# Batch 0 of a sparse attention and MoE kernel, taken pair by pair, with its loads cut to match and a few planned steps moved

## The chip, the cores and the metric

The kernel runs on one core of one Trainium2 chip. The metric is device time in microseconds of one execution (us); lower is better. Engines are named as the profile does: PE (matrix multiplication), PEld (PE's weight loads), DVE (vector), ACT (scalar, with the exponential and logarithm), POOL (GpSimd, which also issues most of the loads) and SP (which issues the stores and some transposes). DMA engines move data between HBM and on-chip memory.

## The reference, cut to what matters

An attention with two kinds of masks, then a two-layer MoE block without routing.

```python
batch, n_heads, seq, head_dim = (8, 8, 576, 64)
stride = 32
rel = pos[:, None] - pos[None, :]
mask_local = (rel >= 0) & (rel < stride)                     # heads 0 to 3
mask_strided = (rel >= 0) & (pos[None, :] % stride == pos[:, None] % stride)   # heads 4 to 7
scores = np.where(masks, scale * q @ k.T, -1e9)
attn = softmax(scores)
x = (attn @ v)  # heads side by side: 4608 tokens x 512
h = x @ w_in            # 512 x 2048
g = np.maximum(h, 0.0) ** 2
out = g @ w_out         # 2048 x 512, float32
```

All inputs are float32 in HBM; the kernel computes in bfloat16, and the loads that POOL issues change the type on the way.

## The kernel before, in words

**Tiles.** Heads go in pairs: a unit u = 4 * batch + pair is two heads of one batch. Pairs 0 and 1 are local, pairs 2 and 3 strided. The attention's output for pair p of all batches lies transposed in `xt[p]` (128 rows = two heads of 64, one column for each of the 4608 tokens). The MoE then runs over nine chunks of 512 tokens. For a chunk, `mm1(c, ff)` (L740) makes one of 16 blocks ff of the hidden layer: four matmuls, one for each pair kk, against `w_in_b`, summed in one bank of PSUM; ACT applies the ReLU, DVE squares. `mm2` (L843) multiplies the squares by `w_out_b` in quarters: part 0 needs the first quarter of w_out, part 1 the second, and so on.

**The order of work is written by hand.** Every engine runs its own instructions in program order. First comes a set-up (L975 to L1015), then batch 0 as the list of words `BATCH0` (L18), each run by `run_step` (L879), then the groups: one group is one `mm1` (four matmuls) or four matmuls of `mm2`, and `PLAN` (L23) says which words of the attention of later batches are put ahead of which group. Groups 0 to 4 are empty, since their blocks were made in batch 0's list; groups 5 to 15 are blocks ff 5 to 15 of chunk 0, groups 16 to 31 its `mm2` (16 to 19 with the first quarter of w_out, 20 to 23 with the second), and from 32 on chunk 1.

**The words that matter here.** A number after a slash gives the PSUM banks.
- `c0q`: change the type of a local pair's q or k on ACT (a), DVE (v) or POOL (g); `T0q`: six transposes on PE and a copy.
- `W0q0`: transposes of the strided q or k of batch 0 in two halves (12 transposes of 96 rows each and a copy, L343 to L352); for later batches (`W1q0`, L334) eight transposes of 72 rows.
- `b2.0`: a bias that carries the mask, written to PSUM by PE (L512); `S2.0`: half of a pair's scores (L542) and the exponential on ACT (L546).
- `N2`: the row sums of a strided pair by PE, then ACT's logarithm and exponential (L660 to L664); `O2`: its product with V and DVE's multiplication into `xt` (L674, L676).
- `H0`: a shift of 32 rows in local V (L447); `D0`: a local pair's product with V, DVE's reciprocal and multiplication (L689 to L696); `E0`: transposes and a copy into `xt` (L729, L732).
- `P0.01`: the matmuls of `mm1` for pair 0 and blocks ff 0 and 1. All 20 matmuls of blocks 0 to 4 are done in this way, in the order of pairs 0, 2, 1, 3.
- `z`: DVE makes the wide local mask for later batches; `w1`: a matmul on nothing, to keep PE warm.
- Of the plan: `l` loads a local q or k, `r` a strided one of batch 1, `V` local V, `U` strided V (two loads), `o` a quarter of w_out, all issued by POOL; `m` are fills by POOL; `s1.x` strided scores of batch 1, `x1.x` its sums and products with V (L617): first the sum with `ones_bd` (L622), then eight or six products with `vb` (L625); `B10`, `B11` spread strided V into `vb` (L434); `D4.0` one half of unit 4's product with V (L699).

**The loads.** SP loads pair 0's q and k. All other loads are issued by POOL, one after another, and go through one queue. Before the change they are: strided q (L324), strided k, pair 1's q and k (L306), local V (L440), strided V (L649), w_in in four parts (L462; blocks ff 0 to 4 for pairs 0 and 2, the same for pairs 1 and 3, blocks 5 to 10, blocks 11 to 15), then those of the plan.

Batch 0 is done with the two local and the two strided pairs interleaved: strided scores before pair 1's, and outputs of pairs 0 and 1 before those of 2 and 3.

Of the kernel before, what the change touches and what calls it, by code (L numbers as in the profile page):

```python
# [9 lines left out]
BF16 = mybir.dt.bfloat16  # L10
# [16 lines left out]
4: r1k V1  # L27
5: o1 U1 mbg
6: o2 l2k8+9 mv0g o3 mk0g
10: c4qv  # L30
11: c4kv
12: l2q8+9 T4qa c5qv
# [135 lines left out]
def kernel(  # L168
# [21 lines left out]
    NBS = 2 * NJ  # L190
    VP = 72
    SR = 80
    NP2 = STRIDE // 2
# [22 lines left out]
    strTs = {nm: rows.enter_context(tc.tile_pool(name=f"strT{nm}", bufs=n, side="right")) for nm, n in (("q", 2), ("k", 1))}  # L216
# [26 lines left out]
    ident = singles.tile([128, 128], BF16)  # L243
# [31 lines left out]
    st = {}  # L275
# [40 lines left out]
    NP3 = 4 * SP_ // QL  # L316
    str_rows = {}

    def load_str_rows(b, name):
        src = q if name == "q" else k  # L320
        if b == 0:
            c = 4 if name == "q" else 8
            t = w_out_b[0:QL, c:c + NP3, :]
            nc.gpsimd.dma_start(out=t, in_=src[b, 4:8].rearrange("h (p j) d -> (h p) (j d)", j=NJ)  # L324
                                .rearrange("(s p) c -> p s c", p=QL))
        else:
            t = str_rows_t[name][0:SP_]
            nc.gpsimd.dma_start(out=t, in_=src[b, 4:8].rearrange("h (m r) d -> (h m) (r d)", r=STRIDE))
        str_rows[b, name] = t

    def step_TS(b, name, g, copy):
        src = str_rows[b, name]
        pt = bank("pt").bitcast(BF16)[:, 0:S]
        if b:  # L334
            for i in range(NJ):
                c = 128 * (NJ * g + i)
                nc.tensor.transpose(pt[:, SP_ * i:SP_ * (i + 1)], src[:, c:c + 128], ident[0:SP_, 0:SP_])  # L337
            if g == 0:
                o = strTs[name].tile([128, NP2 * SR], BF16, name=f"{name}T_s")
                str_T[b, name] = o.rearrange("c (a p) -> c a p", p=SR)  # L340
            copy(str_T[b, name][:, NJ * g:NJ * (g + 1), 0:SP_], pt.rearrange("c (a p) -> c a p", p=SP_))
            return
        for i in range(2):  # L343
            for s3 in range(NP3):
                c = 128 * (2 * g + i)
                o = S // 2 * i + QL * s3
                nc.tensor.transpose(pt[:, o:o + QL], src[:, s3, c:c + 128], ident[0:QL, 0:QL])
        if g == 0:
            o = strTs[name].tile([128, 2 * NJ * SR], BF16, name=f"{name}T_s")
            str_T[b, name] = o[:, 0:2 * NJ * SP_].rearrange("c (a r) -> c a r", a=NJ // 2)  # L350
        o = str_T[b, name]
        copy(o[:, 2 * g:2 * g + 2, :].rearrange("c a r -> c (a r)"), pt)  # L352
        if g == 1:
            for i in range(2):
                st.setdefault(2 + i, {})[name + "T"] = \
                    o[:, :, 2 * SP_ * i:2 * SP_ * (i + 1)].rearrange("c a (h p) -> c h a p", h=2)

    str_T = {}

# [77 lines left out]
    def load_v_local_sw(b):  # L437
        i = (2 * b) % NV
        t = vl_all[:, i:i + 2]
        nc.gpsimd.dma_start(out=t[32:128, :, :, :, 0:D].rearrange("p u h t d -> p (u h t) d"),  # L440
                            in_=v[b, 0:4].rearrange("h (t p) d -> p (h t) d", p=QL))
        for u in range(2):
            st.setdefault(4 * b + u, {})["v"] = t[:, u]
# [13 lines left out]
            st.setdefault(4 * b + u, {})["v"] = t[:, u]  # L457

    def load_w_in(i):
        f = slice(*((0, 640), (0, 640), (640, 1344), (1344, 2048))[i])  # L460
        c = (slice(0, 4, 2), slice(1, 4, 2), slice(0, 4), slice(0, 4))[i]
        nc.gpsimd.dma_start(out=w_in_b[:, c, f], in_=w_in_v[:, c, f])  # L462

    def load_w_out(i):
# [182 lines left out]
    def load_v0():  # L647
        load_v_local_sw(0)
        nc.gpsimd.dma_start(  # L649
            out=vs0.rearrange("p u n d -> p (u n d)").rearrange("p (h c) -> p h c", h=4),  # L650
            in_=v[0, 4:8].rearrange("h (p j) d -> p h (j d)", j=NJ))

    def step_N(u):
        e, hw = st[u]["e"], S // 2
# [217 lines left out]

    idle = xt[0][:, T - 512:T]

    def first_part(kks, ffs):
        for ff in ffs:
            mm1(0, ff, kks, FIRST, None if ff < 2 else "py")

    def run_step(word):  # L879
        word, _, at = word.partition("/")  # L880
        places[:] = [int(x) for x in at.split(",") if x]
        op, arg = word[0], word[1:]
        if op == "w":
            warm(int(arg))
        elif op == "c":
            cast_qk_local(int(arg[:-2]), arg[-2], ENG[arg[-1]])
        elif op == "T":
            step_T(int(arg[:-2]), arg[-2], ENG[arg[-1]])
        elif op == "W":
            step_TS(int(arg[0]), arg[1], int(arg[2]), ENG[arg[3]])  # L890
        elif op == "S":
            u, _, half = arg.rstrip("!").partition(".")
            step_S(int(u), int("!" in arg), [int(half)] if half else range(2))
        elif op == "G":
            step_G(int(arg))
        elif op == "b":
            step_B(*(int(x) for x in arg.split(".")))
        elif op == "N":
            step_N(int(arg))
        elif op == "O":  # L900
            step_O(int(arg))
        elif op in "sx":
            (step_SS if op == "s" else step_XX)(*(int(x) for x in arg.split(".")))
        elif op == "k":
            step_K(int(arg[0]), int(arg[1]), ENG[arg[2]])
        elif op == "m":
            memset_later(arg[:-1], nc.gpsimd if arg[-1] == "g" else nc.vector)
        elif op == "D":
            if "." in arg:
                u, part = arg.split(".")  # L910
                step_D(int(u), int(part))
            else:
                step_D0(int(arg))
        elif op == "E":
            step_E(int(arg.rstrip("av")), ENG.get(arg[-1]))
        elif op == "P":
            first_part(*([int(x) for x in y] for y in arg.split(".")))
        elif op == "H":
            shift_v_local(int(arg[:-1]), ENG[arg[-1]])
        elif op == "C":  # L920
            load_str_tall(int(arg[:-1]), arg[-1])
        elif op == "Q":
            load_qk_rows(int(arg[:-1]), arg[-1])
        elif op == "X":
            transpose_str(int(arg[:-1]), arg[-1])
        elif op == "A":
            transpose_cast(int(arg[:-1]), arg[-1])
        elif op == "R":
            order_local(int(arg[:-2]), arg[-2], ENG[arg[-1]])
        elif op == "Y":  # L930
            transpose_local(int(arg))
        elif op == "V":
            (load_v_local_sw if int(arg) > 2 else load_v_local_all)(int(arg))
        elif op == "U":
            load_v_str(int(arg))
        elif op == "B":
            spread_v_str(int(arg[0]), int(arg[1]), ENG[arg[2]])
        elif op == "l":
            load_qk_local_sw(int(arg[0]), [int(x) for x in arg[2:].split("+")], arg[1])
        elif op == "r":  # L940
            load_str_rows(int(arg[0]), arg[1])
# [60 lines left out]
    for i in range(2):  # L1002
# [92 lines left out]
```

## Time and profile before

| | |
|---|---|
| median of 3 runs | 296.94 us (296.74 to 297.06) |
| the profiled execution: time | 297.07 us |
| its span, first to last instruction | 295.2 us |
| busy: PE, DVE, ACT, POOL | 286.3, 210.5, 170.7, 83.0 us |
| instructions | 5895 |
| read from HBM, written | 37.22 MB, 9.44 MB |

A row of the timeline gives the start in us from the span's start, the duration, engine, line, operation, what it writes `<-` what it reads, shape and count (merged instructions: the duration is from the first's start to the last's end); in brackets the idle time of the engine just before, and what ended it. A row of the chain of waits gives start, duration and what ran. A row of the DMA view names a load, its size as it lands (KB) and the median time from issue to landing. The times of the profiled execution lie 1.87 us above its span; the rest of the execution is outside of all instructions.

### The profile page before, as it was taken

Reading aid. Unit: us, or ns where it says so; the run is one execution under the profiler, and the core shown is the slowest. Engines: PE = TensorE matmul, PEld = TensorE weight load, DVE = VectorE, ACT = ScalarE, POOL = GpSimd, SP = SyncE. Lnnn points to the kernel's source line nnn. Section 1 sums busy time; section 2 is a strip of 40 time slices with the busy share of each in tenths; the row PEclk is TensorE's granted clock in tenths of the full one; section 3 lists DMA queues with packets and bytes.
Section 4 is the critical chain, followed back from the end, with each engine's and each line's share of the span. In section 5 each row is a group of like instructions: output and inputs, shape, how many; then the busy total and the mean of one; then the engine's idle time right before and its main releaser. Section 6 shows DMA issues by size and latency. Waiting matters only on the chain.

```text
span 295.2 us, 5895 instructions
## 1 busy us (share of the span) xinstructions
PE 286.3 (97%) x2177; PEld 155.7 (53%) x2212; DVE 210.5 (71%) x553; ACT 170.7 (58%) x321; POOL 83.0 (28%) x123
## 2 busy tenths in 40 slices
PE   7899999999999999999999999999999999999995
PEld 3554555545545454554454445544454444894594
DVE  6557687697666759678367835675489969968983
ACT  3758846775668736774577447645665466307610
POOL 8874743004513008119303800000000013102300
PEclk9999999999999999999999999999999999999999
DMA  7999999999999999999999999411011110021003
GB/s 149 188 207 204 192 198 190 150 204 215 147 138 213 117 163 201 136 166 141 216 159 147 165 186 147 83 56 73 36 23 52 58 54 0 1 104 42 0 2 142
DMA packets 91724, 37.38 MB, mean 127 GB/s; under 512 B 77548, under 2 KB 85830, under 8 KB 91696
## 3 DMA queue, kind: packets, MB, share of 16 engines
q0 software_dynamic: 50608, 18.33, 57.2%
q1 hardware_dynamic: 40944, 18.62, 34.3%
q8 instruction: 17, 0.28, 0.4%
q14 instruction: 11, 0.09, 0.1%
q10 hardware_dynamic: 144, 0.07, 0.1%
HBM read 37.22 MB, written 9.44 MB: 158 GB/s over the span
## 4 chain that ended last, share of the span: by engine, by line
PE 94%; DMA 2%; issue 1%; DVE 1%; ACT 0%; POOL 0%; DVEq 0%; POOLq 0%
PE psb L748 42%; PE psb L854 33%; PE psb L824 9%; DMA w_out_b<-in_k_dram 2%; PE psb L707 2%; PE psb L625 1%; PE psb L611 1%; PE psb L622 1%; PE psb L587 1%; PE psb L542 1%; PE psb L490 1%; PE psb L729 0%; PE psb L512 0%; PE psb L337 0%; DVE x_l L696 0%
## 5 line engine op out<-in xcount | busy, mean ns | idle before, releaser
L748 PE MATMUL psb<-xt,w_in_b 128*128 128x512 bf16 x557 | 131.7, 379 | 1.1
L754 ACT ACTIVATE r<-psb 128x512 bf16<-128x512 f32 x144 | 85.4, 599 | 47.2 <-PE psb L748 41.8
L854 PE MATMUL psb<-w_out_b,g_sb 128*128 128x512 bf16 x432 | 100.9, 379 | 1.1 <-issue 0.5
L748 PEld LDWEIGHTS <-w_in_b 128*128 128x128 bf16 x576 | 53.2, 97 | 58.3 <-issue 0.9
L758 DVE TENSOR_TENSOR g_sb<-r 128x512 bf16<-128x512 bf16 x112 | 47.1, 423 | 37.0 <-ACT r L754 36.1
L854 PEld LDWEIGHTS <-g_sb 128*128 128x128 bf16 x448 | 41.0, 97 | 44.7
L793 POOL CAST sa<-g_sb 128x256 fp32r<-128x256 bf16 x16 | 9.7, 607 | 100.3 <-DVE g_sb L788 100.3
L638 DVE TENSOR_TENSOR xt<-psb,rv 64x144 bf16<-64x144 f32 x84 | 26.2, 311 | 11.5 <-ACT rv L630 10.4
L858 ACT COPY y<-psb 128x512 f32<-128x512 f32 x28 | 16.6, 592 | 29.4 <-PE psb L854 28.4
L628 ACT ACTIVATE rv<-psb 128x432 f32<-128x432 f32 (+1 forms) x21 | 10.5, 501 | 12.8 <-PE psb L622 12.8
L713 DVE TENSOR_TENSOR x_l<-psb,rinv 96x384 bf16<-96x384 f32 x28 | 15.5, 553 | 1.0
L365 POOL DMA_DIRECT2D q_t<-in_q_dram x6 | 3.4, 569 | 45.3 <-DMA qT_s<-q_t 44.0
L788 DVE TENSOR_TENSOR g_sb<-r 128x512 bf16<-128x512 bf16 x32 | 13.0, 420 | 3.7 <-ACT r L754 3.7
L598 ACT ACTIVATE e<-psb 128x384 bf16<-128x384 f32 x30 | 12.0, 510 | 4.2 <-PE psb L587 4.2
L594 DVE TENSOR_TENSOR e<-e,mask_all 128x576 bf16<-128x576 bf16 x20 | 8.4, 456 | 7.3 <-ACT e L598 7.2
L294 POOL DMA_DIRECT2D k_l<-in_k_dram x16 | 12.2, 765 | 3.6 <-DMA v_st<-in_v_dram 3.6
L612 ACT ACTIVATE e<-psb 128x432 bf16<-128x432 f32 (+1 forms) x21 | 10.4, 496 | 4.0 <-PE psb L611 4.0
L645 DVE TENSOR_TENSOR xt<-psb,rv 64x270 bf16<-64x270 f32 (+1 forms) x28 | 9.8, 425 | 3.7 <-ACT rv L630 3.5
L824 PE MATMUL psb<-t,s 128*128 128x256 f32 x96 | 12.2, 283 | 0.0
L294 POOL DMA_DIRECT2D q_l<-in_q_dram x16 | 11.6, 728 | 0.7 <-DMA k_l<-in_k_dram 0.7
L824 PEld LDWEIGHTS psb<-t,s 128*128 128x128 f32 x96 | 11.6, 189 | 0.0
L630 ACT ACTIVATE rv<-rv 128x432 f32<-128x432 f32 (+1 forms) x21 | 11.2, 532 | 0.7
(135 smaller groups left out, 311.0 us busy)
## 6 DMA issues: line engine op xcount, KB each, us to landing
out_dram<-y SPq DMA_DIRECT2D x35, 256.0 KB, 3.8
w_out_b<-in_moe_w_out_dram POOLq DMA_DIRECT2D x4, 512.0 KB, 15.3
q_t<-in_q_dram POOLq DMA_DIRECT2D x7, 288.0 KB, 7.2
k_t<-in_k_dram POOLq DMA_DIRECT2D x7, 288.0 KB, 6.8
vl<-in_v_dram POOLq DMA_DIRECT2D x6, 288.0 KB, 7.3
v_st<-in_v_dram POOLq DMA_DIRECT2D x7, 216.0 KB, 7.8
w_in_b<-in_moe_w_in_dram POOLq DMA_DIRECT2D x2, 704.0 KB, 13.8
k_l<-in_k_dram POOLq DMA_DIRECT2D x16, 72.0 KB, 7.8
```

The costliest lines, as they stand in the source:

```text
L294: nc.gpsimd.dma_start(out=t[:, :, hh, :], in_=src[b, 2 * p + hh].rearrange("(t p) d -> p t d", p=QL))
L598: nc.scalar.activation(e[:, row, 4 * QL * i:4 * QL * (i + 1)], bk[row][i][:, 0:4 * QL], AF.Exp, scale=scale)
L630: nc.scalar.activation(rv, rv, AF.Exp, scale=-1.0)
L638: nc.vector.tensor_tensor(to[:, :, NJ * part:NJ * (part + 1), par], of, by, op=ALU.mult)
L713: nc.vector.tensor_tensor(x, po[0:QL, :, 0:D], rinv[0:QL].to_broadcast([QL, NL, D]), op=ALU.mult)
L748: nc.tensor.matmul(ph, w_in_b[:, kk, 128 * ff:128 * (ff + 1)], xt[kk][:, 512 * c:512 * (c + 1)], start=(kk == order[0]), stop=(kk == order ...
L754: nc.scalar.activation(r, ph, AF.Relu)
L758: later(1, lambda: nc.vector.tensor_tensor(g[:, ff, :], r, r, op=ALU.mult))
L788: nc.vector.tensor_tensor(g[:, ff, :], r, r, op=ALU.mult)
L824: nc.tensor.matmul(pa, a, b, start=k == 0 and n not in "273", stop=k == 7, skip_group_check=True)
L854: nc.tensor.matmul(py, g[:, ff, 128 * j:128 * (j + 1)], w_out_b[:, ff, :], start=(ff == 0), stop=(ff == 15))
L858: nc.scalar.copy(y, py)
```

## The change

Batch 0's list is written anew: pair 1's q and k come in ahead of the strided ones, scores go pair 0, pair 1, pair 3, pair 2 in half units, then D1, D0, N3, E1, O3, N2, E0, O2, and the 20 matmuls of blocks 0 to 4 are single words `P<pair><block>` in an order that begins with pair 1. The order of the four pairs within a block follows from the list. `z` moves behind most of them and the warming matmuls go. The loads of batch 0 follow a list of their own: strided q, k and V by pairs (two heads on 72 rows), local V by pairs, the two first parts of w_in in exchanged order with pair 2's strided V between them, and the rest of w_in in three parts in place of two. The shift of local V is done by pairs too (`h1`, `h0`).

In the plan `o1` (the second quarter of w_out) goes ahead of `V1` (batch 1's local V), `o3` ahead of the next batch's k, and the words D4, D5, B10, B11, E4 and x1.0 come one or two groups later.

```diff
-FIRST = (0, 2, 1, 3)
+LOADS = "k1 q1 sq3 sk3 sk2 sq2 vl1 vl0 vs3 w1 vs2 w0"
 BATCH0 = """
-    c0qa c0kv T0qa/6 w1/7 T0kv/4 z w1/7 S0/0,2 W0q0v/4 W0q1v/5 b2.0/0 W0k0v/6 W0k1a/7 b2.1/2 b3.0/4 S2
-    c1qv c1kv T1qv/6 T1kv/7 S3.0 b3.1/0 S3.1 b1.0/2 S1.0 b1.1/6 S1.1 H0v D0/4 N2/0 D1/6 E0a/4 N3/2 O2/0
-    P0.01 E1a/6 P0.2/7 P2.012 O3/2 P0.34/0,1 P2.34 P1.01234 P3.0 P3.1 P3.2 P3.3 P3.4
+    c0qa c0kv b1.0/2 T0qa/1 T0kv/6 c1kv S0.1/4 c1qv S0.0/6 T1kv/1 T1qa/5 t3qv/4 b1.1/6 t3kv/0 S1.1 S1.0 t2kv/5
+    b3.1/0 t2qv/4 S3.1 b2.0/2 h1v b3.0/6 h0v S2.0 D1/4 S3.0 b2.1/0 S2.1 D0/2 N3/6 E1v/4 O3/0 N2/6 E0a/2 P10/4
+    P11/5 P14/3 O2/6 P31 P12/0 P33/1 P34 P32 P30 P22 P20 P21 P13 P24 P01 z P00 P02 P04 P23 P03
 """
-4: r1k V1
-5: o1 U1 mbg
-6: o2 l2k8+9 mv0g o3 mk0g
+4: r1k o1
+5: V1 U1 mbg
+6: o2 o3 l2k8+9 mv0g mk0g
...
-19: C2q C2k V2 k11v D4.0
-20: s1.0 D4.1 B10v
-21: s1.1 D5.0
-22: B11v l3k12+13 s1.2 U2
-23: E4a D5.1
-24: x1.0
+19: C2q C2k V2 k11v
+20: s1.0
+21: s1.1 D4.0
+22: D4.1 l3k12+13 s1.2 U2
+23: D5.0 B10v
+24: E4a D5.1 B11v
+25: x1.0
...
+    def load_str_unit(u, name):
+        src = q if name == "q" else k
+        c = (4 if name == "q" else 8) + 2 * (u - 2)
+        t = w_out_b[0:SP_, c:c + 2, :]
+        nc.gpsimd.dma_start(out=t, in_=src[0, 2 * u:2 * u + 2].rearrange("h (p j) d -> p h (j d)", j=NJ))
+        str_rows[u, name, 0] = t
+
+    def step_TU(u, name, copy):
+        src = str_rows[u, name, 0]
+        pt = bank("pt").bitcast(BF16)[:, 0:S]
+        for i in range(NJ):
+            h, a = divmod(i, NJ // 2)
+            nc.tensor.transpose(pt[:, SP_ * i:SP_ * (i + 1)], src[:, h, 128 * a:128 * (a + 1)], ident[0:SP_, 0:SP_])
...
     def load_w_in(i):
-        f = slice(*((0, 640), (0, 640), (640, 1344), (1344, 2048))[i])
-        c = (slice(0, 4, 2), slice(1, 4, 2), slice(0, 4), slice(0, 4))[i]
+        f = slice(*((0, 640), (0, 640), (640, 1024), (1024, 1536), (1536, 2048))[i])
+        c = slice(i, 4, 2) if i < 2 else slice(0, 4)
...
+    def load_v0_local(u):
+        t = vl_all[:, u]
+        nc.gpsimd.dma_start(out=t[32:128, :, :, 0:D].rearrange("p h t d -> p (h t) d"),
+                            in_=v[0, 2 * u:2 * u + 2].rearrange("h (t p) d -> p (h t) d", p=QL))
+        st.setdefault(u, {})["v"] = t
+
+    def shift_v0(u, copy):
+        t = vl_all[:, u]
+        copy(t[0:32, :, 1:NL, 0:D], t[96:128, :, 0:NL - 1, 0:D])
+
+    def load_v0_str(u):
+        nc.gpsimd.dma_start(out=vs0[:, u - 2].rearrange("p (h c) d -> p h (c d)", h=2),
+                            in_=v[0, 2 * u:2 * u + 2].rearrange("h (p j) d -> p h (j d)", j=NJ))
...
-    def first_part(kks, ffs):
-        for ff in ffs:
-            mm1(0, ff, kks, FIRST, None if ff < 2 else "py")
+    parts = [w.partition("/")[0][1:] for w in BATCH0.split() if w[0] == "P"]
+
+    def first_part(kk, ff):
+        mm1(0, ff, [kk], [int(x[0]) for x in parts if int(x[1]) == ff])
...
     load_qk_hw(0)
-    load_str_rows(0, "q")
+    loads = (LOADS + " w2 w3 w4").split()
+    load_first(loads[0])
     make_identity(nc, ident)
-    load_str_rows(0, "k")
+    load_first(loads[1])
...
-    load_qk_local_sw(0, (1,))
-    load_v0()
-    for i in range(4):
-        load_w_in(i)
+    for word in loads[2:]:
+        load_first(word)
```

In the list of loads `k1` and `q1` are pair 1's, `sq3` the strided q of pair 3, `vl1` local V of pair 1, `vs3` strided V of pair 3, `w1` and `w0` the parts of w_in for pairs 1 and 3 and for pairs 0 and 2.

More of the change, by code (lines that the diff above doesn't have):

```diff
@@ L314, in cast_qk_local @@
         s[name] = t
-    NP3 = 4 * SP_ // QL
     str_rows = {}
@@ L320, in load_str_rows @@
         src = q if name == "q" else k
[L321 to L328, printed above, removed]
-        str_rows[b, name] = t
+        t = str_rows_t[name][0:SP_]
+        nc.gpsimd.dma_start(out=t, in_=src[b, 4:8].rearrange("h (m r) d -> (h m) (r d)", r=STRIDE))
+        str_rows[b, name] = t
+    def load_str_unit(u, name):
[10 more added lines that the diff above has]
+            nc.tensor.transpose(pt[:, SP_ * i:SP_ * (i + 1)], src[:, h, 128 * a:128 * (a + 1)], ident[0:SP_, 0:SP_])
+        if (0, name) not in str_T:
+            str_T[0, name] = strTs[name].tile([128, NP2 * SR], BF16, name=f"{name}T_s")
+        o = str_T[0, name][:, S * (u - 2):S * (u - 1)]
+        copy(o, pt)
+        st.setdefault(u, {})[name + "T"] = o.rearrange("c (h a p) -> c h a p", h=2, p=SP_)
     def step_TS(b, name, g, copy):
@@ L333, in step_TS @@
         pt = bank("pt").bitcast(BF16)[:, 0:S]
[L334 to L347, printed above, removed]
-        if g == 0:
[L349 to L356, printed above, removed]
+        for i in range(NJ):
+            c = 128 * (NJ * g + i)
+            nc.tensor.transpose(pt[:, SP_ * i:SP_ * (i + 1)], src[:, c:c + 128], ident[0:SP_, 0:SP_])
+        if g == 0:
+            o = strTs[name].tile([128, NP2 * SR], BF16, name=f"{name}T_s")
+            str_T[b, name] = o.rearrange("c (a p) -> c a p", p=SR)
+        copy(str_T[b, name][:, NJ * g:NJ * (g + 1), 0:SP_], pt.rearrange("c (a p) -> c a p", p=SP_))
     str_T = {}
@@ L645, in step_XX, with load_first @@
                     nc.vector.tensor_tensor(t, of[:, g:, :, lo:lo + k], by[:, g:, :, lo:lo + k], op=ALU.mult)
[L647 to L651, printed above, removed]
+    def load_v0_local(u):
[9 more added lines that the diff above has]
+                            in_=v[0, 2 * u:2 * u + 2].rearrange("h (p j) d -> p h (j d)", j=NJ))
+    def load_first(word):
+        if word[0] == "w":
+            load_w_in(int(word[1]))
+        elif word[0] == "v":
+            (load_v0_local if word[1] == "l" else load_v0_str)(int(word[2]))
+        elif word[0] == "s":
+            load_str_unit(int(word[2]), word[1])
+        else:
+            load_qk_local_sw(0, (int(word[1]),), word[0])
     def step_N(u):
@@ L890, in run_step @@
             step_TS(int(arg[0]), arg[1], int(arg[2]), ENG[arg[3]])
+        elif op == "t":
+            step_TU(int(arg[0]), arg[1], ENG[arg[2]])
+        elif op == "h":
+            shift_v0(int(arg[0]), ENG[arg[1]])
         elif op == "S":
@@ L916, in run_step @@
         elif op == "P":
-            first_part(*([int(x) for x in y] for y in arg.split(".")))
+            first_part(int(arg[0]), int(arg[1]))
         elif op == "H":
```

## The prediction

> **What bounds the kernel now.** I read the page's slices first, then the timeline of the first 50 us, then the DMA view in short windows, last the chain of waits.
>
> ```profile
> PE   7899999999999999999999999999999999999995
> DMA  7999999999999999999999999411011110021003
> ```
>
> PE is busy nine tenths or more of every slice (7.4 us each) but the first two and the last. So an edit to batch 0 can win only what PE idles in front, and keeps it only if nothing later makes PE wait again. The second line warns of that: the DMA engines are full from the second slice to the 25th. Two stretches decide. First, the timeline where the first part of the MoE's first chunk (the 20 matmuls of the P steps) runs, and a row of the chain:
>
> ```profile
> 10.11 0.46 DVE L352 COPY kT_s<-psb 128x576 bf16<-128x576 bf16 x1 [0.98 <-PE psb L347]
> 11.28 3.56 ACT L546 ACTIVATE e<-psb 72x576 bf16<-72x576 f32 x6 [0.35 <-PE psb L542]
> 13.23 0.48 DVE L447 COPY vl<-vl 32x1280 bf16<-32x1280 bf16 x1
> 14.72 0.23 DVE L695 RECIPROCAL rinv<-psb 96x12 f32<-96x12 f32 x1 [1.01 <-PE psb L689]
> 15.03 0.65 ACT L662 ACTIVATE g_sb<-psb 128x576 f32<-128x576 f32 x1 [0.19 <-PE psb L660]
> 15.71 0.68 ACT L664 ACTIVATE g_sb<-g_sb 128x576 f32<-128x576 f32 x1
> 15.86 0.22 DVE L695 RECIPROCAL rinv<-psb 96x12 f32<-96x12 f32 x1
> 16.46 0.64 ACT L732 COPY xt<-psb 128x576 bf16<-128x576 bf16 x1
> 18.80 0.45 PE L674 MATMUL psb<-e,g_sb 72*64 72x72 bf16 x16
> 19.36 0.76 DVE L676 TENSOR_TENSOR xt<-psb,g_sb 128x576 bf16<-128x576 f32 x1 [1.44 <-PE psb L674]
> ...
> 19.25 5.07 PE psb L748 x23
> ```
>
> From 11.28 ACT goes from exponentials (3.56/6 = 0.59 us each) to sums (0.65 + 0.68 a pair) to copies (0.64), and PE's chunk matmuls wait for it. From 19.25 (the chain's row) PE runs through at 5.07/23 = 0.22 us a matmul; 14 of the 20 are after 19.25, so **ff 5 starts at 19.25 + 14 x 0.22 = 22.3**.
>
> Second, the loads. POOL's queue is served in the order of issue; these are issues (timeline) and times to landing (DMA view, windows up to 14 us):
>
> ```profile
> 1.37 0.85 POOL L324 DMA_DIRECT2D w_out_b<-in_q_dram  x1 [0.86 <-POOLq L1079]
> 4.26 0.67 POOL L306 DMA_DIRECT2D xt<-in_q_dram  x1
> 5.65 1.18 POOL L440 DMA_DIRECT2D vl<-in_v_dram  x1
> 6.82 0.75 POOL L649 DMA_DIRECT2D g_sb<-in_v_dram  x1
> 7.57 2.99 POOL L462 DMA_DIRECT2D w_in_b<-in_moe_w_in_dram  x4
> 10.54 0.69 POOL L306 DMA_DIRECT2D xt<-in_q_dram  x1
> 13.54 0.55 POOL L328 DMA_DIRECT2D q_t<-in_q_dram  x1 [0.62 <-DMA vl<-in_v_dram]
> ...
> xt<-in_q_dram POOLq DMA_DIRECT2D x1, 144.0 KB, 6.0
> vl<-in_v_dram POOLq DMA_DIRECT2D x1, 288.0 KB, 7.3
> g_sb<-in_v_dram POOLq DMA_DIRECT2D x1, 288.0 KB, 8.0
> w_in_b<-in_moe_w_in_dram POOLq DMA_DIRECT2D x1, 320.0 KB, 8.8
> q_t<-in_q_dram POOLq DMA_DIRECT2D x1, 288.0 KB, 16.5
> ...
> 30.29 0.51 PEld L337 LDWEIGHTS <-q_t 72*128 72x128 bf16 x8
> ```
>
> Landings: q1 10.3, local V 12.95, strided V 14.8, the first part of w_in 16.4, and batch 1's strided q (q_t) at 13.54 + 16.5 = 30.0. PE takes q_t (W1q0v, group 14) at 30.29. **That load is only 0.25 us early.** Whatever PE wins before it beyond that, it loses waiting there, unless the queue moves up as well.
>
> **Part 1: batch 0 pair by pair.** The three strided loads and local V are halved, w_in is cut in five: 15 issues for 10, the same bytes. At about 0.75 us an issue (2.99/4) POOL is busy 5 x 0.75 = 3.7 us longer, and l1q4, issued at 10.54 before, goes out near 14.2. The row at 13.54 shows what hides that: a load waits for the eighth before it, so some seven are always queued, and q_t takes 16.5 us to land.
>
> What the order costs is at the queue's head. Rows of the DMA view for 2 to 4, 4 to 6, 6 to 8 and 16 to 18 us (packets, MB, share):
>
> ```profile
> q0 software_dynamic: 9, 0.01, 3.6%
> q0 software_dynamic: 271, 0.27, 105.9%
> q0 software_dynamic: 365, 0.34, 115.5%
> q0 software_dynamic: 312, 0.42, 118.2%
> ```
>
> Before 4 us POOL's queue moved 9 packets although its first load was issued at 1.37: some 2.4 us pass before data flows. By 6.0 it had moved 0.28 MB. The new order has only k1 and q1 (2 x 144 KB, 0.295 MB) issued by then, so it is empty at about 6.1; the next load leaves POOL at 4.1 to 4.3, behind the mask operations as q1 did before, and moves from about 6.5. **The queue loses about 0.4 us** (none, if k1 is slow to start; 0.6 at most).
>
> The 72-row halves are the unknown. Strided V, 288 KB on 72 rows, took 14.82 - 12.95 = 1.87 us of the queue; at the rate of the fourth row (0.21 MB/us) it would be 1.42. The three loads that become 72-row halves (strided q, k, V) are 2 x 1.42 + 1.87 = 4.7 us at those prices. Six halves cost 6 x 0.71 = 4.3 if they fill one another's gaps fully, 6 x 0.94 = 5.6 if not at all: -0.4 to +0.9. I take zero: at the third row's 0.17 MB/us, which held while strided q and k moved, the old three come to 2 x 1.73 + 1.87 = 5.3, near the upper end, and some filling closes the rest. So loads of equal position land L = 0.4 later, bounds -0.4 to +1.5.
>
> [...]
>
> Walked through with L = 0.4: the four strided halves, k1 and q1 together have the bytes up to the old k1, which stood 0.7 behind q1's 10.3; so the last half lands at 11.4, local V at 12.4 and 13.4, strided V of pair 3 14.3, w1 15.9, pair 2 16.8, w0 18.4.
> - DVE: h0v waits for 13.4 and takes 0.24 (half of the row at 13.23); then D1 and D0 at 1.14 each (from one reciprocal to the next): to 16.0. E1v's copy as the row at 10.11, with latency 0.5: 16.5, and P10 at **16.8**.
> - ACT: after the last half, transposes and copy, about 0.9, to 12.3; four exponentials to 14.8; N3 1.33 to 16.2; N2 after its matmuls to 17.7; E0a to 18.4; O2's multiply on DVE, 0.76 from 18.0, to 18.8.
> - PE: 20 x 0.22 + 0.45 for O2 = 4.85 from 16.8. P31 is due at 17.9 (pair 3 ready 17.3), P22 at 19.2 (18.8; w0 18.4), P01 at 20.3 (18.4): no hole. **ff 5 at 21.6, 0.7 earlier.**
>
> W0's 48 transposes become 32 and the warming matmuls go; both lie ahead of P10 where PE has holes, and count nothing. "z" on DVE lies ahead of the first squares. w_in's last part lands near 25.4 and is due at 21.6 + 7 x 0.88 = 27.8.
>
> At W1q0v q_t now lands at 30.4; PE would come at 29.6. It starts L - 0.25 = **0.15 us later than before**. The gain in front is spent.
>
> **Part 2: the plan.**
>
> ```profile
> 21.94 0.76 POOL L466 DMA_DIRECT2D w_out_b<-in_moe_w_out_dram  x1 [1.27 <-PE psb L748]
> vl<-in_v_dram POOLq DMA_DIRECT2D x1, 384.0 KB, 16.8
> w_out_b<-in_moe_w_out_dram POOLq DMA_DIRECT2D x1, 512.0 KB, 16.6
> 38.89 1.03 PE L854 MATMUL psb<-w_out_b,g_sb 128*128 128x512 bf16 x4
> ```
>
> Second quarter of w_out: landed 38.5, used 38.89, 0.4 early. Ahead of V (384 KB, about 1.9 us) it lands near 37, V near 38.9 in its place; D4.0, now in group 21, comes at 39.8 or later. Neither waits. The swap saves nothing as long as PE does not come earlier.
>
> The later steps have a price. D5.1 and B11v now stand in group 24, x1.0 in group 25; before, B11v was two groups ahead of x1.0.
>
> ```profile
> 42.32 0.52 DVE L434 COPY vb<-v_st 54x1408 bf16<-54x1408 bf16 x1
> 43.11 0.18 DVE L712 RECIPROCAL rinv<-psb 96x6 f32<-96x6 f32 x1
> 43.33 0.55 DVE L713 TENSOR_TENSOR x_l<-psb,rinv 96x384 bf16<-96x384 f32 x1
> ...
> 42.62 0.86 PE psb L854 x4
> 43.48 0.18 PE psb L622
> ```
>
> After D5.1 PE has four matmuls, 0.86, and x1.0's sum, 0.18; x1.0's products with vb (L625) are due 1.04 us after D5.1's end. On DVE after that end: 0.1 until the reciprocal, 0.7 for both steps, 0.5 for B11v, some 0.1 to PE: 1.4. **PE waits 0.35 us** (0 if DVE's steps overlap more; 0.6 if DVE is behind). Everything of PE stands behind it in its queue.
>
> **The sum** against the profiled execution (297.07 = span 295.2 + 1.87): +0.15 + 0.35 = +0.5. The median of the runs shown is 0.13 lower, 296.94; so **297.4**, +0.17%. About 0.2%, 0.6 us, is what a measurement of this kernel tells from no change.
>
> **Rivals.**
> - **The queue moves up and the gain stays** (faster). Early loads flowed at 0.17 MB/us (third row), not 0.21. If the halves of strided q and k (0.59 MB) run at the later rate, 0.6 is saved, and 0.4 if all six fill their gaps: L = 0.4 - 1.0 = -0.6, q_t at 29.4, and PE wins 0.85. With B11v's wait hidden 296.1, paid 296.45. For: strided V, later in the queue, fits the full rate. Against: the slow rows are the queue's first, whatever stands there. Chance 0.25, of it 0.2 faster.
> - **The halves do not share engines** (slower). L = 0.4 + 0.9 = 1.3: q_t at 31.3, +1.05, and B11v +0.35: 298.3. It decides from L = 0.5, where both waits make +0.6. For: strided V's 1.87. [...] Chance 0.15.
> - **As forecast**, two small waits, 296.9 to 297.9: chance 0.6, of it 0.2 over +0.6.
> [...]
>
> **Numbers.** Predicted 297.4; range 296.2 to 298.3, from the gain kept to the halves unshared, some 0.1 left out on each side. Faster by over 0.2%: 0.2. Within: 0.05 + 0.4 = 0.45. Slower: 0.15 + 0.2 = 0.35.
>
> **What would show it.** In the new trace: the first matmul of L748 near 16.8 and ff 5 near 21.6; q_t landing after 30.2 and PE waiting for it; the second w_out quarter long landed when used, D4.0 without a wait; an idle piece of PE before x1.0's L625 put down to vb. I am wrong if q_t lands before 29.8 (then faster), if ff 5 starts after 22.5 (a wait in batch 0 that I did not see), or if PE waits for V or v_st in groups 21 to 25.

## The result, and the profile after

The changed kernel takes **301.94 us** (median of 4 runs, 301.02 to 305.78) against 297.0 for the kernel before: a ratio of 1.0157, 95% interval 1.0124 to 1.0189. The forecast was 297.4 with a range up to 298.3. It is slower by 1.6%, where +0.17% was forecast. Ratios here and below leave out executions that were disturbed, so a ratio can differ from that of two medians.

The profiled execution is the longest of the four, 305.78 us. Its slices (page, second part; 7.6 us each):

```profile
PE   7898999999949999999999999999999999999995
PEclk9999999999987999999999999999999999999999
DMA  7999999999999999999999999821112110011003
```

Against the rows of before there is one hole in PE, in the twelfth slice, and right behind it a dip of the clock. What PE waited for behind the first 18 us (view of waits, up to 120 us; us in total, times, longest):

```profile
PE psb L763 <- DMA xt<-x_l: 4.0, 1, 4.0
PE psb L487 <- DVE q_l L314: 0.6, 1, 0.6
PE psb L622 <- DVE vb L431: 0.4, 1, 0.4
PE psb L487 <- DVE k_l L314: 0.4, 1, 0.4
```

The first row is what this execution has beyond the others, with a stretch at half clock behind it (windows of 5 us; the granted clock stands behind the engines' busy times):

```profile
85.00:90.00 5.00, 1.05 (x5) 0.31 (x4) 3.17 (x7) 2.78 (x5) 1.43 (x2) 0.86 1.62 102
90.00:95.00 5.00, 5.00 (x12) 1.73 (x12) 0.85 (x2) 1.49 (x3) 0.00 (x0) 0.50 1.72 134
```

The first experiment comes back to it. The other three waits are the change's own. The timeline shows who waits for whom; DVE and PE in turn, then POOL's issue of batch 1's strided q and its time to landing:

```profile
28.27 0.36 DVE L314 COPY q_l<-xt 96x768 bf16<-96x768 bf16 x1 [0.86 <-DMA xt<-in_q_dram]
29.92 0.36 DVE L314 COPY k_l<-xt 96x768 bf16<-96x768 bf16 x1 [0.96 <-DMA xt<-in_k_dram]
...
28.69 0.43 PE L487 MATMUL psb<-ident,q_l 96*128 96x96 bf16 x6 [0.64 <-DVE q_l L314]
30.33 0.43 PE L487 MATMUL psb<-ident,k_l 96*128 96x96 bf16 x6 [0.35 <-DVE k_l L314]
45.88 0.39 PE L622 MATMUL psb<-e,vb 128*128 128x54 bf16 x8 [0.36 <-DVE vb L431]
...
16.88 0.55 POOL L322 DMA_DIRECT2D q_t<-in_q_dram  x1 [0.30 <-POOL q_t L990]
...
q_t<-in_q_dram POOLq DMA_DIRECT2D x1, 288.0 KB, 14.4
```

POOL's queue is late: batch 1's local q and k land when DVE starts on them, 28.25 and 29.9 (before 26.67 and 27.98), and strided q lands at 16.88 + 14.4 = **31.3** (before 30.0, forecast 30.4). So PE already waits two groups ahead of the place the prediction named. The 0.36 us before x1.0's products stands where it was forecast (0.35).

Most other executions of the same kernel look different. The kernel once more (`same_again`), windows of 5 us: PE, PEld, DVE, ACT, POOL busy (instructions), then the granted clock, DMA share, GB/s; and the kernel before in two of them:

```profile
5.00:10.00 5.00, 4.14 (x73) 2.93 (x71) 3.47 (x7) 2.82 (x5) 5.00 (x7) 1.00 1.03 131
10.00:15.00 5.00, 4.21 (x60) 2.94 (x60) 2.13 (x6) 2.32 (x5) 4.87 (x7) 0.72 1.51 147
15.00:20.00 5.00, 4.89 (x59) 3.05 (x59) 2.97 (x5) 3.50 (x6) 4.19 (x6) 0.50 1.22 196
20.00:25.00 5.00, 4.89 (x32) 2.15 (x32) 0.76 (x1) 1.18 (x3) 4.36 (x5) 0.76 1.25 207
```

```profile
5.00:10.00 5.00, 3.81 (x55) 2.55 (x54) 2.42 (x6) 1.88 (x3) 4.98 (x7) 1.00 1.30 168
10.00:15.00 5.00, 4.92 (x91) 3.16 (x89) 3.27 (x8) 4.16 (x7) 4.26 (x6) 1.00 1.57 196
```

PE reads as busy through most of it, but **its clock fell to a half from 12.2 to 22.4 us** (the column behind the engines: 0.72, 0.50, 0.76; in these windows busy time is that of slowed matmuls: four matmuls of the chunk take 1.91 us at half clock, at 23.35 in `small_first`, and 1.03 at full clock, at 35.65 there). Behind it PE waits for no load at all, since it comes 3.4 us late itself:

```profile
31.63 0.43 PE L487 MATMUL psb<-ident,q_l 96*128 96x96 bf16 x6
```

This is PE's first work for batch 1's local q (block ff 12); in the kernel before it starts at 28.25. The row makes a good milestone: it parts what PE loses ahead of it, in front, from what it waits for behind it. (ff 5, forecast at 21.6 and a sign of being wrong after 22.5, starts at 22.05 in the first profile and at 25.7 in this one; before at 22.4.) The mean clock of a whole execution tells the two kinds apart: it was 0.977 to 0.983 in six of the eight executions of the changed kernel. Of the other two, one is the first profile (0.989), and one, 302.45 us at 1.0, has none.

### The profile page after: what moved, and what is told of

Same layout as the page of the kernel before. It is cut to its first block, busy times and chain, and to the rows that moved or that the text cites. A ratio compares the mean times of both kernels' runs of the same rounds, so it can differ in the third digit from the quotient of the medians.

```text
span 303.8 us, 5912 instructions
## 1 busy us (share of the span) xinstructions
PE 289.9 (95%) x2183; PEld 156.4 (51%) x2218; DVE 211.5 (70%) x555; ACT 170.4 (56%) x320; POOL 86.0 (28%) x128
## 4 chain that ended last, share of the span: by engine, by line
PE 82%; DMA 10%; POOL 4%; issue 2%; DVE 1%; ACT 0%; DVEq 0%; SPq 0%; POOLq 0%
PE psb L763 38%; PE psb L869 27%; PE psb L839 9%; DMA xt<-x_l 5%; DMA xt<-in_k_dram 5%; PE psb L722 2%; PE psb L608 1%; POOL w_in_b L459 1%; PE psb L622 1%; PE psb L584 1%; PE psb L619 1%; POOL w_out_b L329 1%; PE psb L487 1%; POOL vl L646 1%; PE psb L539 1%
## 5 line engine op out<-in xcount | busy, mean ns | idle before, releaser
L763 PE MATMUL psb<-xt,w_in_b 128*128 128x512 bf16 x557 | 134.5, 384 | 5.1 <-DMA xt<-x_l 4.0
L625 ACT ACTIVATE rv<-psb 128x432 f32<-128x432 f32 (+1 forms) x21 | 10.5, 501 | 12.6 <-PE psb L619 12.6
L839 PE MATMUL psb<-t,s 128*128 128x256 f32 x96 | 12.2, 283 | 0.0
## 6 DMA issues: line engine op xcount, KB each, us to landing
w_out_b<-in_moe_w_out_dram POOLq DMA_DIRECT2D x4, 512.0 KB, 14.8
```

What stands on the lines that cost most here:

```text
L763: nc.tensor.matmul(ph, w_in_b[:, kk, 128 * ff:128 * (ff + 1)], xt[kk][:, 512 * c:512 * (c + 1)], start=(kk == order[0]), stop=(kk == order ...
L839: nc.tensor.matmul(pa, a, b, start=k == 0 and n not in "273", stop=k == 7, skip_group_check=True)
```

## The experiments

Three theories stood after this. **The halves**: the 72-row loads cost the queue time, the recorded slow rival. **The clock**: the new list leaves PE so little to do early on that its clock falls, and the queue does not matter. **The gap**: the thinner head of the queue (k1 and q1, then nothing) is what makes it late. The table has all runs; milestones in us from each profile: "k" is the landing of batch 1's local k, "q_t" that of its strided q, "ff 12" PE's first work for its local q (the wait right before it left out), "waits" what PE waits for from there up to 50 us. A wait ahead of ff 12 is not in the last column; it shows in ff 12.

| kernel | median us (range, runs) | ratio (95%) | profiled: us, clock | k | q_t | ff 12 | waits |
|---|---|---|---|---|---|---|---|
| before | 296.94 | | 297.07, 1.0 | 28.0 | 30.0 | 28.25 | 0 |
| changed | 301.94 (301.02–305.78, 4) | 1.0157 (1.0124–1.0189) | 305.78, 0.989 | 29.9 | 31.3 | 28.05 | 1.35 |
| same_again | 301.41 (300.95–302.38, 4) | 1.0148 (1.0124–1.0173) | 301.15, 0.982 | 29.5 | 31.0 | 31.63 | 0.4 |
| old_plan | 301.02 (298.93–304.29, 6) | 1.0120 (1.0088–1.0152) | 298.93, 1.0 | 29.1 | 30.5 | 27.9 | 1.8 |
| new_plan | 297.28 (297.05–302.53, 12) | 0.9996 (0.9971–1.0022) | 297.06, 1.0 | 27.5 | 29.1 | 27.7 | 0.3 |
| head_one | 302.83 (301.2–305.95, 6) | 1.0195 (1.0152–1.0238) | 301.2, 0.982 | 30.75 | 32.2 | 31.7 | 0.4 |
| warm_list | 301.88 (300.38–302.96, 6) | 1.0145 (1.0112–1.0178) | 300.38, 0.998 | 30.4 | 31.8 | 28.6 | 2.5 |
| before_no_warm | 297.47 (296.58–303.5, 12) | 1.0006 (0.9986–1.0026) | 296.86, 0.999 | 28.8 | 30.2 | 28.05 | 0 |
| halves_old_order | 301.52 (300.12–302.61, 4) | 1.0151 (1.0115–1.0186) | 300.12, 0.997 | 30.1 | 31.3 | 28.9 | 1.6 |
| small_first | 304.23 (303.73–304.58, 4) | 1.0228 (1.0200–1.0257) | 304.2, 0.977 | 28.5 | 29.9 | 35.0 | 0.4 |
| half_qk | 299.84 (299.08–304.05, 6) | 1.0080 (1.0061–1.0099) | 300.29, 0.994 | 30.75 | 31.6 | 31.4 | 0 |
| half_v | 298.33 (296.94–303.83, 12) | 1.0041 (1.0016–1.0066) | 303.48, 0.994 | 27.7 | 29.25 | 28.3 | 0.4 |
| half_v_again | 300.11 (297.57–304.24, 10) | 1.0026 (1.0009–1.0042) | 298.12, 0.998 | 28.7 | 29.8 | 27.8 | 0.3 |
| five_w_in | 297.14 (297.01–297.58, 11) | 0.9994 (0.9979–1.0008) | 297.26, 1.0 | 28.7 | 30.1 | 28.1 | 0.2 |
| whole_loads | 298.19 (297.8–306.08, 9) | 1.0031 (1.0019–1.0042) | 298.3, 1.0 | 29.0 | 30.2 | 29.1 | 0.4 |
| half_qk48 | 298.16 (297.31–303.81, 12) | 1.0033 (1.0011–1.0056) | 297.31, 0.999 | 28.55 | 30.3 | 28.3 | 0 |
| after48 | 301.56 (300.86–304.73, 6) | 1.0172 (1.0133–1.0212) | 301.76, 0.982 | 29.75 | 31.1 | 31.5 | 0.4 |
| after48_warm | 298.99 (298.54–300.61, 6) | 1.0069 (1.0048–1.0091) | 298.8, 0.999 | 29.15 | 30.2 | 28.4 | 1.1 |

**1. The kernel once more** (`same_again`, no edit).

> The changed kernel as it is, for a second profile and more times. Its first profile has three losses: PE waits 1.2 us for batch 1's local q and k (groups 10 to 13), 0.4 us for vb before x1.0, and near 86 us 4.0 us for the transposing DMA that brings unit 9's output into xt, after which the granted clock is 0.5 for 5 us. If the third is what sets runs apart, this profile shows the first two again at about the same size, and the third with another one; if the time is 301 to 302 with no third loss, the theory of three losses is wrong.

Measured: 301.41 us, without the 4 us hole, without the waits for q and k, and with the clock at a half in front. By its own terms the theory of three losses was wrong. So the hole at 85 us is a thing of single executions. In the first profile it came from one of SP's transposes of `x_l` into `xt` (issue, and time to landing; that profile first, then before):

```profile
74.14 3.82 SPq L737 DMA_TRANSPOSE xt<-x_l  x1
...
xt<-x_l SPq DMA_TRANSPOSE x1, 15.6
```

```profile
70.68 1.26 SPq L722 DMA_TRANSPOSE xt<-x_l  x1
...
xt<-x_l SPq DMA_TRANSPOSE x1, 8.1
```

It landed at 89.8 instead of 78.8. A like row stands in `half_v`'s profile (1.7 us, and 2.1 for a transpose of q_t). Why these transposes are late at times is not settled.

**2. The two halves of the change apart** (`old_plan`: the changed kernel with the plan of before; `new_plan`: the kernel before with the changed plan).

> Batch 0 and its loads as changed, the plan as before (second quarter of w_out behind V1, D4 to x1.0 at the old groups). Queue theory (the new loads make POOL's queue 1.3 to 1.9 us late, everything else follows): the waits for local q and k stay at 1.2 us, the wait for vb goes (0.4 us), a wait for the second quarter of w_out may come, and the late transposes stay: 300 to 302 us. Plan theory (the later steps of the plan make the late loads late): no wait near 86 us, 297.5 to 298.5 us.

> Batch 0 and its loads as before, only the plan as changed. Queue theory: the queue is on time, so only the wait for vb before x1.0 is paid, 0.3 to 0.4 us: 297.3 to 297.5 us, and the transposes of unit 9 come in time. Plan theory: most of the loss is here, 300 us or more, with PE waiting near 86 us.

The plan alone is no loss that can be measured, 0.9996, though its profile has the wait for vb:

```profile
PE psb L626 <- DVE vb L435: 0.3, 1, 0.3
```

That it is paid is seen, what it comes to in the total is inside the interval. Nearly all of the loss comes with batch 0 and its loads. And with the late queue the old plan is no better by more than the intervals allow (1.0120 against 1.0157): in its profile PE waits for the second quarter of w_out, which the changed plan had brought forward:

```profile
PE psb L868 <- DMA w_out_b<-in_moe_w_out_dram: 1.5, 1, 1.5
```

**3. The gap at the head** (`head_one`: the first strided half is issued right behind q1, ahead of the masks).

```diff
     load_first(loads[1])
+    load_first(loads[2])
...
-    for word in loads[2:]:
+    for word in loads[3:]:
```

> The changed kernel with the first strided load (sq3) issued right behind q1, ahead of the mask operations on POOL, so that the queue is not empty between q1 and sq3; the masks come 0.7 us later. Gap theory (the queue is late because it ran empty at its head): batch 1's local k lands 0.5 to 0.8 us earlier than 29.9 and the wait of PE in groups 10 to 13 falls from 1.2 to about 0.5 us. Halves theory (the 72-row halves are slow in themselves): it lands less than 0.3 us earlier.

With the gap filled q_t lands at 32.2, later than ever. **The gap theory falls** as the cause of the late queue. The 0.4 us that the prediction took for the gap is not seen at q_t in `small_first` either (29.9, experiment 5).

**4. The clock kept up** (`warm_list`: eight matmuls on zeros in the changed list; `before_no_warm`: the two warming steps, one matmul each, taken out of the list before, as the change does).

```diff
-... T0qa/1 T0kv/6 c1kv S0.1/4 c1qv S0.0/6 T1kv/1 T1qa/5 t3qv/4 b1.1/6 t3kv/0 S1.1 S1.0 t2kv/5
+... T0qa/1 T0kv/6 w2/0 c1kv S0.1/4 c1qv S0.0/6 w1/0 T1kv/1 T1qa/5 w2/0 t3qv/4 b1.1/6 w2/0 t3kv/0 S1.1 S1.0 w1/1 t2kv/5
```

> The changed kernel with eight matmuls on nothing put where PE waits in batch 0's list (two behind T0k, one behind S0, two ahead of t3q, two ahead of t3k, one ahead of t2k). Clock theory (in most executions of the changed kernel the granted clock falls to 0.5 at about 12 us for 10 us, because PE does too little in the 3.4 us before; that costs some 4 us in front): the clock stays at 1.0 and the time falls to 298 to 299.5 us, with the waits for batch 1's local q and k (1.2 us) and for vb (0.4 us) left. Queue theory alone (the time is lost to late loads, the clock only follows): no gain over 0.5 us, 301 us.

> The kernel before without its two warming matmuls in batch 0's list, which the change removes as well. If these two alone keep the clock up: the granted clock falls near 12 us in most executions, 300 us or more. If the thin stretch comes from the new order's waits: clock 1.0, 297.0 to 297.3 us.

The clock stayed up (0.994 to 1.0 in all six) and **the time did not move**, 301.88. Its profile has the waits in place of the slow stretch:

```profile
PE psb L869 <- DMA w_out_b<-in_moe_w_out_dram: 1.6, 1, 1.6
PE psb L487 <- DVE k_l L314: 0.7, 1, 0.7
PE psb L487 <- DVE q_l L314: 0.2, 1, 0.2
```

So the clock theory alone falls too: behind the one wall stands another of like height. The first row is w_out's third quarter, landed at 46.4. This profile, at 300.38, is the fastest of the six; what the median has beyond it, 1.5 us, no trace shows. And in the list of before the two warming matmuls are not needed: 1.0006 without them, clock 0.999.

**5. The order, and the halves** (`halves_old_order`: list order, loads' order and plan of before, but with all the cuts; `small_first`: the kernel before with k1 and q1 as the first loads, strided q and k whole behind them).

```diff
-LOADS = "k1 q1 sq3 sk3 sk2 sq2 vl1 vl0 vs3 w1 vs2 w0"
+LOADS = "sq3 sq2 sk3 sk2 q1 k1 vl1 vl0 vs3 vs2 w0 w1"
```

```diff
-    load_str_rows(0, "q")
+    load_qk_local_sw(0, (1,), "k")
     make_identity(nc, ident)
-    load_str_rows(0, "k")
+    load_qk_local_sw(0, (1,), "q")
...
-    load_qk_local_sw(0, (1,))
+    load_str_rows(0, "q")
+    load_str_rows(0, "k")
```

> The order of work, of loads and the plan as before, but the strided loads and local V in halves by pairs and w_in in five parts, as in the change, with the change's transposes of 72 rows. Halves theory (72-row halves leave DMA engines idle): batch 1's local k lands 0.9 to 1.5 us later than before's 27.5 to 28.0, and PE waits 0.6 to 1.2 us for it: 297.8 to 298.5 us. Gap theory (the queue only ran empty at its head in the change): it lands within 0.3 us of before, 297.0 to 297.4 us.

> The kernel before with pair 1's k and q loaded first and the strided q and k, whole as before, behind the mask operations: the change's order at the head of the queue, without its halves. Gap theory: batch 1's local k lands 0.4 to 0.9 us later than before's 27.5 to 28.0, and the strided scores, for which PE now waits, move batch 0's end 1 to 2 us later: 298 to 299 us. Halves theory: it lands within 0.3 us of before.

In the old order the cuts alone cost the whole 1.5%, more than either forecast, with q_t at 31.3, the changed kernel's own value. The order alone leaves q_t where it was (29.9). Its local k, 28.5, lies in the range of the gap theory, but k lands at 28.7 to 28.8 in `before_no_warm` and `five_w_in` too, without any gap. What `small_first` loses lies ahead of ff 12 (35.0 against 28.25): PE waits 1.9 and 0.9 us for strided q and k, and the clock is at a half from 12.0 to 25.7 us. It still has the two warming matmuls of before.

**6. Which cuts** (`half_qk`, `half_v`, `half_v_again`, `five_w_in`: the kernel before with one kind of cut each). The edits are those of the change, for strided q and k, for local and strided V, and

```diff
-        f = slice(*((0, 640), (0, 640), (640, 1344), (1344, 2048))[i])
+        f = slice(*((0, 640), (0, 640), (640, 1024), (1024, 1536), (1536, 2048))[i])
```

> The kernel before with one edit: strided q and k come in four 72-row halves instead of two 96-row loads (their transposes in four steps of 8 instead of four of 12); V, w_in, order and plan as before. If the 72-row halves themselves cost the queue, each 72-row load a like amount (six halves together moved batch 1's local k from 27.5 to 28.8 to 29.1 to 30.8), these four take about two thirds: local k at 29.0 to 29.6, and some 299.5 to 300.5 us. If a smaller first load at the queue's head is what counts (rival), all of it is here: 30.0 and 301.5. If V's halves are the cost, 28.0 and 297.1.

> The kernel before with one edit: local V and strided V of batch 0 come in halves (one pair each) instead of whole. If each 72-row half costs a like amount: local k at 28.5 to 29.0 and 298 to 299 us, since strided V was on 72 rows already and only its number of loads doubles. If the cost sits in the strided q and k alone (rival): 27.5 to 28.3 and 297.1.

> half_v once more, for a profile without the late transposes. If V's halves cost by the queue: local k and strided q of batch 1 later than before's 28.0 and 30.0. In the profile of half_v they were not (27.7 and 29.25), so rather: no load behind 25 us is late, the vb wait or a late transpose by SP's queue is there, 297.5 to 299 us.

> The kernel before with one edit: w_in in five parts instead of four, the same bytes. These loads are on 128 rows. If only the 72-row loads cost the queue: 27.5 to 28.3 and 297.1 us. If every load more costs it (rival), a fifth of the five added loads: local k at 28.4 and 298.

One more load of 128 rows costs nothing (0.9994), though POOL issues its later loads 0.6 to 1.8 us later. V's halves cost 0.3 to 0.4%, but not through the place of later loads (q_t 29.25 and 29.8); by what, is open. Strided q and k cost most, 0.8%, and push local k to 30.75 (forecast 29.0 to 29.6) and q_t to 31.6.

But PE does not pay for it there: the last column is 0, and the 3.2 us of this profile lie wholly ahead of ff 12. Strided V and the first part of w_in stand behind the halves in the queue. They land at 17.7 and 18.7 (before 14.8 and 16.4), PE waits, and the chunk's first matmul starts 1.6 us late (`half_qk`, then before):

```profile
18.75 0.60 PE L768 MATMUL psb<-xt,w_in_b 128*128 128x512 bf16 x2 [0.53 <-DMA w_in_b<-in_moe_w_in_dram]
...
17.15 0.38 PE L748 MATMUL psb<-xt,w_in_b 128*128 128x512 bf16 x1
```

The other 1.6 us go with the clock, which is at a half from 19.4 to 22.9 us (0.71 from 20 to 25). Three other executions, at 0.999 to 1.0, took 299.1 to 300.1, so most of the loss does not need the low clock.

**7. The rows of the halves** (`half_qk48`: `half_qk` with each half on 48 rows of three pieces instead of 72 of two; the same loads, bytes and pieces of 1 KB).

```diff
-        c = (4 if name == "q" else 8) + 2 * (u - 2)
-        t = w_out_b[0:SP_, c:c + 2, :]
-        nc.gpsimd.dma_start(out=t, in_=src[0, 2 * u:2 * u + 2].rearrange("h (p j) d -> p h (j d)", j=NJ))
+        c = (0 if name == "q" else 6) + 3 * (u - 2)
+        t = w_out_b[0:48, c:c + 3, :]
+        nc.gpsimd.dma_start(out=t, in_=src[0, 2 * u:2 * u + 2].rearrange("h (p j) d -> (h p) (j d)", j=NJ)
+                            .rearrange("(s p) c -> p s c", p=48))
```

> half_qk (the kernel before, strided q and k in four halves) with one edit: each half lies on 48 rows of 3 tokens' groups instead of 72 rows of 2, so that 16 divides the rows; the same bytes and as many loads; its transposes are 12 of 48 rows instead of 8 of 72. If the 72 rows are the cost: batch 1's local k at 28.0 to 28.8 (half_qk 30.75, before 27.5 to 28.8) and 297 to 298 us (half_qk 299.84). If it is the number or the size of the loads (rival): local k near 30.5 and some 299.8 us.

As the halves theory said: k 28.55, and 298.16 us (forecast 297 to 298); q_t lands at 30.3, and the ratio is 1.0033 instead of 1.0080. The 0.3% that remain are not explained. The profiles side by side, 72 rows first (POOL's issues, time to landing, windows of 2 us):

```profile
8.60 0.76 POOL L661 DMA_DIRECT2D g_sb<-in_v_dram  x1
14.92 0.56 POOL L321 DMA_DIRECT2D q_t<-in_q_dram  x1 [0.29 <-POOL q_t L995]
...
g_sb<-in_v_dram POOLq DMA_DIRECT2D x1, 288.0 KB, 9.1
q_t<-in_q_dram POOLq DMA_DIRECT2D x1, 288.0 KB, 16.7
...
10.00:12.00 2.00, 1.76 (x41) 1.36 (x37) 1.34 (x5) 1.26 (x3) 2.00 (x4) 1.00 1.95 131
12.00:14.00 2.00, 1.97 (x35) 1.02 (x33) 1.62 (x3) 1.97 (x5) 1.96 (x4) 1.00 1.31 138
```

```profile
7.70 0.76 POOL L663 DMA_DIRECT2D g_sb<-in_v_dram  x1
14.03 0.55 POOL L321 DMA_DIRECT2D q_t<-in_q_dram  x1 [0.29 <-POOL q_t L997]
...
g_sb<-in_v_dram POOLq DMA_DIRECT2D x1, 288.0 KB, 7.0
q_t<-in_q_dram POOLq DMA_DIRECT2D x1, 288.0 KB, 16.2
...
10.00:12.00 2.00, 1.87 (x44) 1.40 (x40) 1.21 (x4) 1.29 (x3) 2.00 (x3) 1.00 2.06 157
12.00:14.00 2.00, 1.97 (x34) 1.04 (x34) 1.97 (x3) 1.96 (x4) 1.70 (x3) 1.00 1.19 169
```

Strided V lands at 8.60 + 9.1 = 17.7 behind the 72-row halves and at 7.70 + 7.0 = 14.7 behind the 48-row ones: 3 us. In the two windows shown the DMA engines read about as busy either way (1.95 and 1.31 against 2.06 and 1.19), so that 72-row halves leave them idle, as the expectation of `halves_old_order` has it, is not shown; but they move 131 and 138 GB/s behind the 72-row halves and 157 and 169 behind the 48-row ones. Of strided V's 16 completions behind the 72-row halves the trace has the last two at 15.7 and 17.7, so the last is 2 us behind the one before it. What waits for a load starts behind its last: in the changed kernel's trace batch 1's local q has the last two of its 16 at 27.62 and 28.25, and DVE starts on it at 28.27. The first part of w_in, behind strided V in the queue of `half_qk`, has its last two at 17.5 and 18.7. POOL also issues strided V 0.9 us later (8.60 against 7.70); `five_w_in` had later issues as well, and they cost nothing.

**8. The two walls taken down, one and both** (`after48`: the changed kernel with that same edit; `after48_warm`: and the matmuls of `warm_list`).

> The changed kernel with the same edit: strided q and k's four halves on 48 rows; strided V's two halves stay on 72. If the 72 rows are the cost of the queue: strided k of pair 2 and strided q of pair 2 some 0.5 to 1 us earlier, local k at 28.6 to 29.2 instead of 29.5 to 29.9. Its time falls to 299 to 300 if the clock is kept, and stays near 301 if the clock falls to a half for three windows as before, since PE itself is then behind. If the number of loads is the cost: local k at 29.5 to 30, no change.

> after48 with eight matmuls on zeros in batch 0's list, which kept the clock in warm_list. If the late queue and the clock are the two limits and nothing else is: 297.5 to 299 us. If the queue stays late (rival): 300 to 302 as warm_list.

| changed kernel | as changed | warming matmuls |
|---|---|---|
| 72-row halves | 301.94 | 301.88 |
| 48-row halves | 301.56 | 298.99 |

**Neither alone moves the time; both together take 2.9 us off.** With the clock kept, the 48 rows move the queue: q_t 30.2 instead of 31.8, local k 29.15 instead of 30.4, w_out's third quarter 44.65 instead of 46.4, and PE's waits are 1.1 instead of 2.5. With the clock low they hardly do: in `after48` k lands at 29.75, in the range recorded for "no change", and q_t at 31.1; its time, 301.56, is the one forecast for a low clock. Why the queue stays late there is open. In `after48` the clock falls (0.972 to 0.983 in all six):

```profile
15.00:20.00 5.00, 4.78 (x58) 2.84 (x55) 2.43 (x5) 3.57 (x6) 4.07 (x5) 0.50 1.24 203
```

What is left of `after48_warm`, 0.7%, has one row up to 50 us, again w_out's third quarter, landed at 44.65 (before 42.5):

```profile
PE psb L871 <- DMA w_out_b<-in_moe_w_out_dram: 1.1, 1, 1.1
```

**9. The new order with whole loads** (`whole_loads`: the list with warming matmuls and the plan of the change; strided q and k on 96 rows, V whole, w_in in four).

> The changed kernel with its order of loads, its list for batch 0 (with eight matmuls on zeros that keep TensorE active) and its plan, but with the loads whole as before: strided q and k on 96 rows, local V and strided V whole, w_in in four. If the halves are what the change loses by: local k at 28.0 to 28.5, no matmul behind 22 us waits over 0.4 us for a load, 296.5 to 298 us. If the order of the loads and the thinner start count by themselves (rival; k1 and q1 first in the kernel before gave 304.2 with the clock at half speed for a stretch): over 300 us, with the clock low in the profile or the queue late again.

298.19, 1.0031, just above the forecast: no wait for a load behind 22 us and q_t 30.2, though local k, at 29.0, is later than forecast. ff 12 at 29.07 is 0.8 later than before's 28.25, and 0.36 for vb comes on top. In front PE's transposes of strided k start at 11.1 us, when it lands (before 9.6), and its first matmul of the chunk at 18.2 (before 17.15): whole strided loads seem too late for the new list, but no run tests that alone. No version here beats the kernel before.

## Why the prediction was wrong

- **The step that failed is L**, "I take zero" for the six halves, "loads of equal position land L = 0.4 later". With strided q and k in 72-row halves q_t lands at 30.5 to 32.2 in seven profiles (mean 31.4), with them whole or on 48 rows at 29.1 to 31.1 in eleven (mean 30.0; only `after48` is above 30.3). In the changed kernel L was 1.3 (31.3 against 30.0), and the shift grew: w_out's third quarter landed 1.8 later (44.3 against 42.5). The recorded slow rival ("the halves do not share engines", L = 1.3, q_t at 31.3) named the halves and had q_t to 0.1 us; it got a chance of 0.15. That it hit so closely is in part luck: 0.4 of its 1.3 was the gap, which no run bears out, and the halves alone cost more than its 0.9 (+1.6 in `half_qk`, +1.3 in `halves_old_order`). The zero rested on an estimate from two rates of the queue (0.17 and 0.21 MB/us) and on "some filling" of gaps; no run shows the filling. `half_qk` measures +1.6 us on q_t and 0.8% with 72 rows, `half_qk48` +0.3 and 0.3% with 48 rows, the same bytes and as many loads. What makes the 72-row halves late, the traces do not show.
- **What a late queue costs was too small as well.** The rival priced 1.05 us at q_t. The runs show waits for batch 1's local q and k (1.0 in the changed kernel) and, in their place or on top of them, 1.1 to 1.6 for a quarter of w_out (`old_plan`, `warm_list`, `after48_warm`); in `half_qk` the cost lies in front, at w_in. "Neither waits" held for the second quarter and for V; the third quarter was not priced.
- **The clock was not thought of.** The prediction took the warming matmuls out at no cost, since they lie "where PE has holes", and counted the 20 matmuls at 0.22 us each. In six of eight executions of the changed kernel the clock fell to a half; in the profile of `same_again` the 20 matmuls run from 19.3 to 25.7, and ff 12 is 3.4 us late. The two warming matmuls that the change takes out are not shown to be the reason: the old list does without them, and `small_first`, which keeps them, fell in all four. What held the clock in the new list was eight.
- **The gain in front, 0.7, is not there.** P10 at 17.00 (forecast 16.8) is near, but ff 12 comes at 27.9 to 28.05 with the new list at full clock (28.4 and 28.6 with the warming matmuls), at 27.7 to 28.3 in seven profiles with the list of before and its strided q and k in time. The profile that the sum was made against lies at the late end of that spread.
- **vb was right**: 0.36 for 0.35. Where PE waits for w_out instead (`warm_list`, `after48_warm`), the wait for vb is gone.
- **The sums close to some 0.5 us** in most profiles. `same_again`: 31.63 - 28.25 = 3.4, and 0.4 for vb, 3.8 of 301.15 - 297.07 = 4.1. `warm_list`: 0.35 + 2.5 = 2.9 of 3.3. The first profile: -0.2 + 1.35 + 3.95 and some 3.4 for the 6.8 us at half clock (88.6 to 95.5), 8.5 of 8.7. `half_qk`: 3.2 of 3.2. In `halves_old_order` they explain 2.2 of 3.05. These are profiled executions; the medians of `warm_list` and `halves_old_order` are 1.4 to 1.5 us above theirs.

## What to carry to other kernels

Before a load is cut, compare the rows of its pieces: the same bytes in as many loads cost the queue about 1.3 us on q_t with 72 rows (31.6) that 48 rows did not cost (30.3). When one remedy does nothing, try it with the other one in place: here two limits of like height hid each other, and only the four kernels of the table showed both. And read the granted clock by stage before believing a busy PE, above all where an edit makes PE wait for loads early on.

## What the runs showed of the hardware

- **The clock falls while PE is far from idle.** In `same_again` it falls at 12.2 us, and in the 3.41 us ahead (8.77 to 12.18) PE reads 2.36 us busy; in `after48` it falls at 12.6, and PE reads 4.37 us busy from 5 to 10. In the kernel before it stays at 1.0 over a stretch of the same 3.41 us with less, 2.22 (6.50 to 9.91), and in `before_no_warm` over 3.56 from 5 to 10. So busy time alone does not decide; what does, no run here shows.
- **The stretches at half clock come in four lengths.** By the granted clock of the windows they last 3.5 us in `half_qk` (19.4 to 22.9), 6.8 in the first profile (88.6 to 95.5), 10.2 to 10.3 in `same_again` (12.2 to 22.4), `head_one` (12.1 to 22.4) and `after48` (12.6 to 22.9), and 13.7 in `small_first` (12.0 to 25.7): about one, two, three and four times 3.4 us. The 3.4 us in the expectation of `warm_list` is this length, and the three windows in that of `after48` are three of it.
